# Three chained models in one kernel: masks moved between PE and DVE by batch, weights converted in another order, every step placed anew

## The chip, the cores and the metric

The kernel runs on 1 core of one Trainium2 chip. The metric is the device time of one execution in microseconds. Before the change it is 1239.44 us (median of 3 runs, 1238.56 to 1243.17).

## The reference

Attention over 4 batches, 8 heads, 576 tokens and 64 dims feeds two MLPs over the 2304 tokens. Cut to what is computed:

```python
scores = scale * np.matmul(q, k.transpose(0, 1, 3, 2))
thresh = np.max(scores, axis=-1, keepdims=True) - tau
scores = np.where(scores >= thresh, scores, -1000000000.0)
attn = np.exp(scores - np.max(scores, axis=-1, keepdims=True))
attn = attn / (np.sum(attn, axis=-1, keepdims=True) + 1e-09)
x = np.matmul(attn, v)                      # -> 2304 x 512
h = x @ w_in                                # 512 x 2048
P = a[0] + a[1] * h + a[2] * h**2 + a[3] * h**3
Q = 1.0 + np.abs(b[0]) * np.abs(h) + np.abs(b[1]) * h**2
y = (P / (Q + 1e-06)) @ w_out               # 2048 x 512
out = ((y @ w1) * (y @ w2) @ w3) @ w_out2   # 512x1024, 512x1024, 1024x1024, 1024x512
```

## The kernel before, in words

**Tiles.** Heads are taken in pairs `c` (4 to a batch). The 576 queries of a pair are cut into five blocks `blk` of 128 rows (the last holds the 64 remaining rows of both heads); `s` is the head of the pair. So a batch `b` has 36 score tiles of 128 x 576, and the kernel 144. A half `u` of a pair is blocks 0 and 1 or blocks 2 to 4.

**A score tile.** `qk` (PE, L446, L441) makes the scores in PSUM, `top` (DVE, L455) their row maximum, `thr` (DVE, L462) the threshold. The mask is then made in one of two ways. By PE: `below` (ACT, L469) writes a large Relu for each score under the threshold, `drop` (PE, L476) subtracts it in PSUM by two matmuls with the constant `minus`, and `exp` (ACT, L491) exponentiates and sums. By DVE: `exp` (ACT, L486) exponentiates everything, and one DVE instruction (L488) compares, multiplies and sums. `MASK = (1, 3)` gives blocks 1 and 3 of every batch to DVE, the others to PE. `recip` (POOL L502, then DVE L504) makes the factor 1/sum. `p_hi` and `p_lo` split the probabilities into two float16 parts `hl`: for `s == 1` ACT first multiplies by the factor (L509), a copy rounds and a plain subtraction, mostly on POOL (L301), gives the rest; for `s == 0` rounding and subtraction carry the factor, and the subtraction is then a scalar_tensor_tensor on DVE (L298). `p_t` transposes both parts by DMA, `pv` (PE, L545) multiplies by V.

**Weights.** The 72 weight tiles come in as 64-bit floats. `conv_w` makes float32 of a tile in three DVE instructions (L621, L624, L627). `split_w` makes two float16 parts of the tiles of `w_in`, `w_out`, `w1`, `w2` and of W. W is `w3` times `w_out2`, made once: `w_product` (PE, L873) for each of 8 row tiles from all 8 tiles of `w_out2` (`wo2`) and two of `w3`.

**MLPs.** The 2304 rows are 9 groups of 256. For each group `mlp1` runs 8 steps: `h_product` (PE, L761), `act_h` (ACT), `num` (DVE, L780, L782), `den` (POOL), `inv` (ACT), `quotient` (DVE, L798 to L802, last part POOL), `y_product` (PE, L818). The group's end is `y_evac` and `square` of y (ACT, L679, `sq<-yf`). `mlp2` runs 4 steps of `ab_product` (PE, L925), `a_copy`, `c_mul` (L937), `o_product` (PE, L957). The ninth group is made of the last 64 queries of each batch.

**Order.** Every step is an event with a number, in the order in which `merge` lists them. `ORDER`, a string of event numbers, says in which order the events' instructions are emitted; a generator event is resumed at each further mention of its number, and a letter behind a number gives an engine (`a` ACT, `p` POOL, `v` or none DVE) where there is a choice. Each engine executes its own instructions in this order and waits at semaphores for the others. DMAs are all issued by SP. Buffers are few: 2 score tiles `S` in PSUM (a third of batch 0's scores use `y` as well), 2 of `h`, 1 of `y`.

Of the kernel before, what the change touches and what calls it, by code (L numbers as in the profile page):

```python
# [36 lines left out]
96 158 99a 130 139 110 139 101p 98 112 139 109 102 142 110 169 144 112 134 144 113 132a 113 135 120
137 138 237 150 140 150 141 143 150 115a 145 161 180 161 153 155 116 161 118 120a 239a 172 121p 238
172 164 172 166 123 146 183 245 183 175 160 183 177 148 162 253 163 186 149 149 188 165 151a 188 156
191 152 124 156a 191 154 167 157p 168 167 126a 159 168 187 194 126 194a 170 189 197 194p 170 190  # L40
197a 171a 192 197p 176 173 199 184 176a 199v 174 240 199p 193 178v 202 196 240 179 195 202p 240 200
198 202p 185v 260 205 214 205a 241 215 201 205p 217 243 218 208 203 181 203 208a 204v 206 209 208p
209a 248 207 248 182a 211p 210 182 248 210a 212 213 210p 268 250 213v 255 213p 220 255 216 220 216a
255 242 222 216p 276 219 222 219a 244 223 258 219p 223 246 225a 247 229 226 221 228 229a 221v 263
221p 224 231v 224a 263 233 227 224p 263 227a 230 227p 283 266 230v 230p 232 232a 235 232p 234 235a
271 271 271 278 291 278 249 235p 278 251 252 286 298 236a 286 254 256 236 286 257 270 293 306 273
293 259 292 281 259 261v 318 262 265 265a 272 264 288 274 267p 277 275 293 279 269 277 313 296 279
402 294 280 406 280 295 282a 301 412 301 287 284 412 287a 297 301 289p 285 308 299 321 303 308 290
300 308 302 320 316 329 311 316 302 316 304a 322 336 319 305 323 307 315 325 324 327 324 328 330 324
333 332 331 393 331 326 348 331 335 339 344 334 339 370 337 337 339 338a 350 317a 396 343 413 340  # L50
343a 352 342 341 345p 346 346 395 346 398 351 353 400 372 349 404 373 355 406 406 309 357 355 375
310 357 312 310 354 358 401 354 376 347 314a 354 405 403 314 414 358 356 436 360v 425 407 362 365
436 365a 359 363 410 410 378 367p 415 410 380 368 380 417 381a 418 383 421 385 410 422 409 410 424
426 429 428 432 446 416 434 471 449 416 434 450 435a 452 441 473 441a 438 411a 443p 475 439 419 455
419 456 505 455 477 456 416 479 440 458 359 507 359 423p 440 458 444 407 361 407 361a 460p 508 386
364 388 361p 511 364a 388 390 366 408 408 364p 366a 445 408 369 366p 369a 462 437 371 512 463 444
369p 371a 374 391v 391 371p 374a 461 377 374p 377a 461 379 377p 379a 420 420 420 448 382 379p 382a
384 382p 384a 387 387a 384p 389 389a 431 431 431 459 387p 392 392a 389p 394 394a 392p 397 397a 394p
399 399a 442 442 442 453 470 453 453 465 482 465 465 476 493 476 476 487 504 487 397p 487 466 499
497 466a 499 399p 480 499 467p 514 510 572 510 517 518 510 483 469 427 520 483 583 427 484v 486 500a  # L60
430 488 522 500 524 539 430 532 440 525 430 563 447p 525 464 528v 501 515 529 533 430p 541 531 533a
515 542 451 535p 545 546 565 515 548 546 451 548 503a 515 567 464 550 454 569 550 454 552a 597 454
521a 570 577 558 454p 490 577 558a 491 577 573 494 491 559p 589 544 527 589 574 433 464 537 589 433
496a 472p 553 590 496 433 556 574 474 576v 594 579 474 468 580 594 468 562 478 478 594 591a 478 599
478p 594 601 603 591 604 457 457 600a 538 611 538 605 457 538 607 582 549 622 586 549 584 549 584
555 587a 657 587 555 555 659a 555 659 481 651 560a 617 617 481 566 617 628 481 662 628 485 628 485
690 509 489 489 492 509 489 492 495p 608 513 610 634 612 593 516 516 498 595p 634 498 614 502 634
502 513 615 513 502 519p 629 502v 615 506 618a 631 506 523 632 624 620 506 523 635 634 621 624a 526
636 625p 526 638 534 526 639a 627 636 526p 534 645 638 557 656 536 641 656 536 530 540 536 530 540
543p 641 656 642a 530 667 648 701 557 644 547 667 646 547 648p 665 661 649p 667 561 673 551 561 725  # L70
# [164 lines left out]
def tile_attention_mlps(  # L235
# [258 lines left out]
    def by_dve(blk):  # L494

        return blk in MASK

# [673 lines left out]
```

## Time and profile before

| | |
|---|---|
| median of the runs | 1239.44 us |
| the profiled execution's own time | 1243.93 us |
| its span | 1242.2 us |
| busy: PE, DVE, ACT, POOL | 1011.8 (81%), 898.0 (72%), 756.1 (61%), 445.4 us (36%) |
| granted TensorE clock, mean | 0.912 of 2.4 GHz |
| moved by DMA | 120.37 MB, mean 97 GB/s |

The busy shares are means over a program whose stages differ: the first has weights to convert, the last has only MLP work. So the rows below cut the span at the ends of MLP1 groups, which can be found in the trace (`sq<-yf` on ACT) and in the order of the steps.

### The profile page before, as it was taken

To read this page: it belongs to the slowest core of one execution; us is meant where nothing else is said; L and a number is where in the kernel's file an instruction comes from. 1 tells how busy PE (TensorE), PEld (TensorE's weight loads), DVE (VectorE), ACT (ScalarE), POOL (GpSimd) and SP (SyncE) were. 2 spreads that over 40 slices of the span, in tenths; PEclk is the share of its full clock that TensorE was granted. 3 is DMA by queue.
4 is the path that set the end of the run, shared out by engine and by line. 5 is a ranking of instruction groups with operands and counts; after the bars stand their busy time and mean duration, and the time that the engine had idled before them with its cause. 6 is when DMAs were issued, how large, how long until landed. Compare 5 with 4: busy or idle time off the path is not lost. (4 is left out here: it accounts for less than half of the span.)

```text
span 1242.2 us, 20722 instructions
## 1 busy us (share of the span) xinstructions
PE 1011.8 (81%) x7940; PEld 748.2 (60%) x7940; DVE 898.0 (72%) x1623; ACT 756.1 (61%) x1266; POOL 445.4 (36%) x425
## 2 busy tenths in 40 slices
PE   2463553998987767579999888799989999999997
PEld 1232432565565545357767766687767777878774
DVE  5899979868897989988858767974388533756710
ACT  5587784555767767677766555664467544544521
POOL 1145155223242644445433433443234321423311
PEclk9855665999998878779999989999999999999998
DMA  7875855635643246533481334123323331000000
GB/s 213 257 186 150 219 137 174 168 87 139 161 122 73 63 111 149 133 76 72 81 207 47 84 80 109 30 53 71 71 56 64 65 67 29 2 18 18 1 18 17
DMA packets 201443, 120.37 MB, mean 97 GB/s; under 512 B 176384, under 2 KB 180480, under 8 KB 201344
## 3 DMA queue, kind: packets, MB, share of 16 engines
q1 hardware_dynamic: 201344, 119.05, 39.1%
q8 instruction: 62, 1.02, 0.4%
q14 instruction: 37, 0.30, 0.1%
HBM read 69.21 MB, written 7.34 MB: 62 GB/s over the span
## 5 line engine op out<-in xcount | busy, mean ns | idle before, releaser
L818 PE MATMUL y<-gg,wp 128*128 128x256 f16 x1728 | 212.7, 280 | 32.2 <-POOL gg L301 17.4
L818 PEld LDWEIGHTS <-wp 128*128 128x128 f16 x1728 | 171.0, 100 | 71.7 <-issue 48.1
L761 PE MATMUL h<-xp,wp 128*128 128x256 f16 x1536 | 187.2, 282 | 30.0 <-DVE U L782 19.3
L761 PEld LDWEIGHTS <-wp 128*128 128x128 f16 x1728 | 172.8, 101 | 63.0 <-DVE U L782 21.5
L925 PEld LDWEIGHTS <-wp 128*128 128x128 f16 x1728 | 169.5, 98 | 32.4 <-issue 5.9
L301 POOL TENSOR_TENSOR A<-A,r 128x512 f32<-128x512 f32 x71 | 96.0, 1352 | 130.3 <-ACT r L775 124.4
L301 POOL TENSOR_TENSOR gg<-A,r 128x512 f16<-128x512 f32 x61 | 84.8, 1390 | 126.9 <-DVE A L802 108.8
L446 PE MATMUL S<-raw 64*128 64x288 f32 x472 | 106.2, 492 | 28.7 <-ACT p L491 15.5
L301 POOL TENSOR_TENSOR hl<-p,hl 128x576 f16<-128x576 f32 x62 | 86.6, 1397 | 119.5 <-ACT hl L285 92.4
L455 DVE TENSOR_REDUCE m<-S 128x1 f32<-128x576 f32 x132 | 95.6, 748 | 27.7 <-PE S L446 15.9
L957 PE MATMUL y<-wp,gg 128*128 128x512 f16 x432 | 102.7, 384 | 4.0 <-POOL gg L301 1.9
L301 POOL TENSOR_TENSOR gg<-U,gg 128x512 f16<-128x512 f32 x36 | 42.9, 1191 | 151.0 <-ACT gg L285 140.6
L502 POOL TENSOR_SCALAR su<-su 128x2 f32<-128x2 f32 (+1 forms) x80 | 25.0, 313 | 200.7 <-ACT p L491 137.7
L446 PEld LDWEIGHTS S<-raw 64*128 64x128 f32 x472 | 57.7, 215 | 61.1 <-ACT p L491 20.1
L768 ACT ACTIVATE U<-h,cf 128x512 f32<-128x512 f32 x72 | 55.7, 773 | 58.6 <-PE h L761 27.0
L925 PE MATMUL h<-yy,wp 128*128 128x256 f16 x768 | 91.0, 277 | 0.1
L298 DVE SCALAR_TENSOR_TENSOR hl<-p,su,hl 128x576 f16<-128x576 f32 x80 | 79.0, 988 | 15.4 <-ACT hl L287 14.6
L469 ACT ACTIVATE x<-S,th 128x576 bf16<-128x576 f32 x73 | 51.4, 735 | 44.9 <-DVE th L462 41.7
L301 POOL TENSOR_TENSOR wp<-cw,wp 128x512 f16<-128x512 f32 x53 | 72.7, 1388 | 13.2 <-ACT wp L285 6.2
L798 DVE SCALAR_TENSOR_TENSOR gg<-U,cf,r 128x512 f16<-128x512 f32 x72 | 59.5, 827 | 20.8 <-ACT r L792 20.0
L957 PEld LDWEIGHTS <-gg 128*128 128x128 f16 x432 | 41.4, 99 | 51.4 <-issue 5.2
L624 DVE SCALAR_TENSOR_TENSOR cw<-rw,cw 128x512 int32<-128x512 int32 x72 | 69.2, 962 | 2.1
(185 smaller groups left out, 1947.7 us busy)
## 6 DMA issues: line engine op xcount, KB each, us to landing
rw<-in_moe_w_dram SPq DMA_DIRECT2D x32, 512.0 KB, 4.3
rw<-in_moe_w_out_dram SPq DMA_DIRECT2D x24, 512.0 KB, 3.9
raw<-in_k_dram SPq DMA_DIRECT2D x32, 288.0 KB, 3.8
wr<-in_v_dram SPq DMA_DIRECT2D x16, 576.0 KB, 4.5
rw<-in_moe_w_in_dram SPq DMA_DIRECT2D x16, 512.0 KB, 4.4
wr<-in_v_dram SPq DMA_DIRECT2D x16, 320.0 KB, 4.5
out_dram<-A SPq DMA_DIRECT2D x16, 256.0 KB, 2.1
raw<-in_q_dram SPq DMA_DIRECT2D x16, 160.0 KB, 3.4
```

What stands on the lines that cost most here:

```text
L298: nc.vector.scalar_tensor_tensor(o, x, scale, hi, op0=ALU.mult, op1=ALU.subtract)
L301: (nc.gpsimd if eng[0] == "p" else nc.vector).tensor_tensor(o, x, y, op=op)
L446: nc.tensor.matmul(t[s][:, half, :HS], x[r, o:o + 128], y[r, keys], start=True, stop=True)
L455: nc.vector.tensor_reduce(st["m", b, c, blk][:, s:s + 1], t[:, :, :HS], axis=AX.XY, op=ALU.max, negate=True)
L469: nc.scalar.activation(x, st["S", b, c, blk][s][:, :, :HS], AF.Relu, bias=st["th", b, c, blk][:, s:s + 1], scale=-BIG)
L624: nc.vector.scalar_tensor_tensor(t, r[:, :, 1], -0x40000000, t, op0=ALU.bitwise_and, op1=ALU.bitwise_or)
L761: nc.tensor.matmul(t[:, e, :], w[:, a, o:o + 128], x[:, y, c, :], start=c + i == 0, stop=c == KD - 1 and i == 2)
L768: nc.scalar.activation(u, h, AF.Identity, bias=cf[:, 15:16], scale=cf[:, 0:1])
L798: stt(p[:, 0, :], u, cf[:, 3:4], r, ALU.add, ALU.mult)
L818: nc.tensor.matmul(t[j // 2][:, j % 2, :], w[:, a, 128 * j:128 * j + 128], x[:, y, TG * e:TG * e + TG], start=f + e + i + j % 2 == 0, stop ...
L925: nc.tensor.matmul(t[:, TG * e:TG * e + TG], w[:, a, o:o + 128], x[:, y, c, :], start=c + i == 0, stop=c == KD - 1 and i == 2)
L957: nc.tensor.matmul(st["o", g][kt], x[:, a, m:m + 128], w[:, y, :], start=jp + e + i == 0, stop=jp == 3 and e == 1 and i == 2)
```

## The change

Masks: `MASK` becomes a table by batch. Batch 0 makes all masks by PE, batch 1 as before, batches 2 and 3 all by DVE. `FIRST` does the same for the factor: in batch 0 ACT multiplies it in first for both heads, elsewhere for `s == 1` as before. `thr` and the first part of `recip` go through a helper `small` that takes POOL or DVE from the letter in `ORDER`. The lists given to `merge` are cut elsewhere, and `ORDER` is new in every line: the tiles of `w_out2` and `w3` are converted first, the W products stand in batch 0, and `mlp2` of group 0 stands already beside batch 1.

```diff
 ORDER = """
-59 0 1 3 12 17 2 4 62 5 13p 62 19a 70 21 62 7 64 22 67 24 6 25 27 10 73 28 30 73 8 32 73 33 9 81 9
...
-    MASK = (1, 3)
+    MASK = ((), (1, 3), (0, 1, 2, 3, 4), (0, 1, 2, 3, 4))
+    FIRST = ((0, 1), (1,), (1,), (1,))
...
+    def small(o, i, x, y, f, g):
+        (nc.gpsimd if eng[0] == "p" else nc.vector).tensor_scalar(o, i, x, y, op0=f, op1=g)
...
-        nc.vector.tensor_scalar(th[:, 0:n], m, d1, -1.0 if by_dve(blk) else -BIG,
-                                op0=ALU.add, op1=ALU.mult)
+        small(th[:, 0:n], m, d1, -1.0 if by_dve(b, blk) else -BIG, ALU.add, ALU.mult)
...
-        if by_dve(blk):
+        if by_dve(b, blk):
...
-    def by_dve(blk):
-
-        return blk in MASK
+    def by_dve(b, blk):
+
+        return blk in MASK[b]
...
-        nc.gpsimd.tensor_scalar(su, su, 1e-9, 2.0**-14, op0=ALU.add, op1=ALU.mult)
+        small(su, su, 1e-9, 2.0**-14, ALU.add, ALU.mult)
...
-        if scaled(blk, s):
+        if scaled(b, s):
...
-    def scaled(blk, s):
-
-        return s == 1
+    def scaled(b, s):
+
+        return s in FIRST[b]
...
-    merge(attend(0, 0), wi)
-    a = attend(0, 1); n = len(a) // 2
-    merge(a[:n], wo)
-    merge(a[n:] + attend(1, 0), M((1,0), (1,1)), wa)
-    merge(attend(1, 1), M((1,2)), wb)
+    a = attend(0, 0)
+    merge(a, wa[:len(wa)-27] + wi)
+    b = attend(0, 1)
+    merge(b, wo + M((1,0)))
+    merge(attend(1, 0), M((1,1)), wa[len(wa)-27:]+wb)
     fw_()
-    merge(attend(2, 0), M((1,3),(2,0)))
-    merge(attend(2, 1), M((1,4),(2,1)))
-    merge(attend(3, 0), M((1,5),(2,2),(2,3)))
-    merge(attend(3, 1), M((1,6),(2,4),(2,5)))
-    merge(M((1,7),(2,6),(1,8),(2,7),(2,8)))
+    merge(attend(1, 1), M((1,2),(2,0)))
+    merge(attend(2, 0), M((1,3),(2,1)))
+    merge(attend(2, 1), M((1,4),(2,2)))
+    merge(attend(3, 0), M((1,5),(2,3)))
+    merge(attend(3, 1), M((1,6),(2,4)))
+    merge(M((1,7),(2,5),(1,8),(2,6),(2,7),(2,8)))
```

DVE in batch 0, before, about its third pair: subtraction with the factor (`hl<-p,su,hl`), a conversion (`cw`), a threshold, two masks (`p,su<-S,th,p`).

```order
L298 SCALAR_TENSOR_TENSOR xp<-h,xp 128x256
L504 RECIPROCAL su<-su 128x2
L455 TENSOR_REDUCE m<-S 128x1
L298 SCALAR_TENSOR_TENSOR vl<-wr,vs,vh 128x640
L298 SCALAR_TENSOR_TENSOR hl<-p,su,hl 128x576
L621 TENSOR_SCALAR cw<-rw 128x512
L624 SCALAR_TENSOR_TENSOR cw<-rw,cw 128x512
L627 SCALAR_TENSOR_TENSOR cw<-rw,cw 128x512
L462 TENSOR_SCALAR th<-m,d_86 128x2
L488 SCALAR_TENSOR_TENSOR p,su<-S,th,p 128x576 x2
```

DVE in batch 0 now, about its third pair as well.

```order
L628 SCALAR_TENSOR_TENSOR cw<-rw,cw 128x512
L300 SCALAR_TENSOR_TENSOR xp<-h,xp 128x256
L631 SCALAR_TENSOR_TENSOR cw<-rw,cw 128x512
L508 RECIPROCAL su<-su 128x2
L460 TENSOR_REDUCE m<-S 128x1
L460 TENSOR_REDUCE m<-y 128x1
L306 TENSOR_SCALAR th<-m,d_86 128x2
L625 TENSOR_SCALAR cw<-rw 128x512
L651 TENSOR_REDUCE acc<-h 128x1
```

Subtractions and masks are gone from DVE here; maxima, some thresholds and the conversions are left.

POOL in batch 0, before, from its first instruction on data (`raw` is q; `su` the sums, `hl` the subtraction).

```order
L291 TENSOR_SCALAR raw<-raw,flag 128x256
L502 TENSOR_SCALAR su<-su 128x2
L301 TENSOR_TENSOR hl<-p,hl 128x576
L502 TENSOR_SCALAR su<-su 128x2
L301 TENSOR_TENSOR hl<-p,hl 128x576
```

POOL at the same place now (`th` the thresholds, `qp` the last queries).

```order
L293 TENSOR_SCALAR raw<-raw,flag 128x256
L303 TENSOR_TENSOR hl<-p,hl 128x576 x2
L306 TENSOR_SCALAR su<-su 128x2
L303 TENSOR_TENSOR hl<-p,hl 128x576
L306 TENSOR_SCALAR th<-m,d_86 128x2
L291 CAST hl<-p 128x576
L303 TENSOR_TENSOR hl<-p,hl 128x576 x3
L306 TENSOR_SCALAR th<-m,d_86 128x2
L433 COPY qp<-raw 64x64 x2
```

The subtractions of both heads have come to POOL, and thresholds stand between them.

PE beside batch 2, before: `ab_product` matmuls with a `drop` of two tiles among them.

```order
L925 MATMUL h<-yy,wp 128x256
L476 LDWEIGHTS minus
L476 MATMUL S<-x,minus 128x288
L476 LDWEIGHTS minus
L476 MATMUL S<-x,minus 128x288
L476 LDWEIGHTS minus
L476 MATMUL S<-x,minus 128x288
L476 LDWEIGHTS minus
L476 MATMUL S<-x,minus 128x288
L925 LDWEIGHTS wp
```

PE beside batch 2 now: a `qk` of two tiles among `ab_product` matmuls, and no `drop` anywhere in batches 2 and 3.

```order
L929 LDWEIGHTS wp
L929 MATMUL h<-yy,wp 128x256
L451 MATMUL S<-raw 128x288 x4
L929 LDWEIGHTS wp
L929 MATMUL h<-yy,wp 128x256
```

The four `drop` matmuls of a pair of tiles have left PE's queue; DVE's L492 (L488 before) stands for them.

## Rows read from the trace of the kernel before

**Rows 1.** Timeline of ACT near 555 us: start, duration, instruction.
```profile
555.36 1.06 ACT L679 ACTIVATE sq<-yf 128x1024 bf16<-128x1024 f32 x1
```

**Rows 2.** Busy time by stretch; the header row names the columns.
```profile
core 0: us, PE busy (x) PEld busy (x) DVE busy (x) ACT busy (x) POOL busy (x), PEclk, DMA share, GB/s
0.00:555.40 555.40, 373.51 (x2462) 249.94 (x2463) 474.71 (x865) 374.06 (x652) 212.63 (x209) 0.82 0.57 146
555.40:1242.30 686.90, 638.25 (x5478) 498.24 (x5478) 423.34 (x759) 382.02 (x615) 232.79 (x216) 0.98 0.25 57
```

**Rows 3.** The same view, cut at ends of MLP1 groups.
```profile
425.90:555.40 129.50, 90.98 (x682) 66.11 (x679) 116.40 (x215) 90.74 (x154) 61.89 (x55) 0.80 0.48 117
...
724.40:843.40 119.00, 107.23 (x938) 83.38 (x939) 88.92 (x158) 74.75 (x123) 43.74 (x41) 0.96 0.31 69
843.40:975.70 132.30, 125.86 (x1090) 96.25 (x1087) 81.47 (x155) 80.22 (x131) 44.76 (x47) 0.99 0.29 64
975.70:1103.10 127.40, 125.28 (x1103) 100.59 (x1102) 64.49 (x118) 63.13 (x98) 38.39 (x35) 1.00 0.16 35
```

**Rows 4.** Groups by form, DVE: count | busy us, mean ns | idle before.
```profile
L455 DVE TENSOR_REDUCE m<-S 128x1 f32<-128x576 f32 x132 | 95.6, 748 | 27.7 <-PE S L446 15.9 <-PE S L441 10.1 <-PE y L446 1.5
L298 DVE SCALAR_TENSOR_TENSOR hl<-p,su,hl 128x576 f16<-128x576 f32 x80 | 79.0, 988 | 15.4 <-ACT hl L287 14.6
...
L780 DVE SCALAR_TENSOR_TENSOR U<-h,cf,U 128x512 f32<-128x512 f32 x72 | 53.7, 746 | 21.0 <-ACT A L772 12.4 <-ACT r L775 3.7 <-ACT U L768 3.2
...
L488 DVE SCALAR_TENSOR_TENSOR p<-S,th,p 128x576 f32<-128x576 f32 x59 | 46.8, 812 | 2.4 <-ACT p L486 1.3
...
L462 DVE TENSOR_SCALAR th<-m,d 128x2 f32<-128x2 f32 x64 | 23.2, 363 | 1.5
L291 DVE TENSOR_SCALAR hl<-p,su 128x576 f16<-128x576 f32 x24 | 22.8, 951 | 1.1
...
L298 DVE SCALAR_TENSOR_TENSOR vl<-wr,vs,vh 128x640 f16<-128x640 f32 x16 | 16.9, 1054 | 6.9 <-ACT vh L287 6.9
...
L301 DVE TENSOR_TENSOR gg<-A,r 128x512 f16<-128x512 f32 x11 | 14.6, 1327 | 0.4
...
L301 DVE TENSOR_TENSOR hl<-p,hl 128x576 f16<-128x576 f32 x2 | 3.3, 1642 | 0.0
```

**Rows 5.** Groups by form, DVE: the three conversion lines.
```profile
L624 DVE SCALAR_TENSOR_TENSOR cw<-rw,cw 128x512 int32<-128x512 int32 x72 | 69.2, 962 | 2.1
...
L627 DVE SCALAR_TENSOR_TENSOR cw<-rw,cw 128x512 int32<-128x512 int32 x72 | 61.4, 853 | 1.6
...
L621 DVE TENSOR_SCALAR cw<-rw 128x512 int32<-128x512 int32 x72 | 43.6, 605 | 2.3 <-DMA rw<-in_moe_w_out_dram 1.1 <-DMA rw<-in_moe_w_dram 0.7 <-DMA rw<-in_moe_w_in_dram 0.2
```

**Rows 6.** The same three lines asked for one by one: minimum/median/maximum ns.
```profile
L621 DVE TENSOR_SCALAR cw<-rw x72: 407/421/1500, 8.1 to 523.6; 128x512 int32<-128x512 int32 x72
L624 DVE SCALAR_TENSOR_TENSOR cw<-rw,cw x72: 677/693/3336, 8.6 to 524.0; 128x512 int32<-128x512 int32 x72
L627 DVE SCALAR_TENSOR_TENSOR cw<-rw,cw x72: 668/691/1649, 9.3 to 524.7; 128x512 int32<-128x512 int32 x72
```

**Rows 7.** Groups by form, POOL.
```profile
L301 POOL TENSOR_TENSOR hl<-p,hl 128x576 f16<-128x576 f32 x62 | 86.6, 1397 | 119.5 <-ACT hl L285 92.4 <-issue 17.9 <-DMA out_dram<-A 5.8
...
L289 POOL CAST wp<-cw 128x512 f16<-128x512 f32 x5 | 3.7, 747 | 0.4 <-ACT cw L667 0.3
```

**Rows 8.** Groups by form, PE, from 800 to 1000 us.
```profile
L925 PE MATMUL h<-yy,wp 128*128 128x256 f16 x384 | 44.1, 273 | 0.0
...
L446 PE MATMUL S<-raw 64*128 64x288 f32 x88 | 13.7, 429 | 0.0
L545 PE MATMUL h<-pT,vh 128*64 128x256 f16 x108 | 7.0, 275 | 1.3 <-DVE U L782 1.3
L476 PE MATMUL S<-x,minus 128*128 128x288 bf16 x30 | 5.3, 287 | 0.0
```

**Rows 9.** Waits over the whole span: who waited for whom, us, times, longest.
```profile
PE S L446 <- ACT p L491: 15.5, 4, 14.7
```

More of the change, by code (lines that the diff above doesn't have):

```diff
@@ L37 @@
[L37 to L58, printed above, removed]
@@ L227 @@
[L227 to L230 removed]
+7 0 1 3 12 92 18 2 4 5 13v 22 8 94p 20v 10 15 24 26 27v 6 31 9 14 9 29 9 35 11a 33 17 37 17 11 39 53
+40v 16a 19 40 17 55 42 23 16 42a 48 44p 57 28 48a 59v 61 50p 46 21 63 64 21 68 66 52 21 70 96 25 32
@@ new lines @@
+2287 2297 2291p 2287 2299 2298a 2299 2287 2292 2298 2292 2292 2299 2300 2293a 2299 2293 2299 2300
+2292 2301 2307 2301 2302 2301 2302 2307 2294a 2303p 2294 2314 2308 2304 2309 2314 2304 2309 2305
+2369 2308 2305 2308 2305 2328 2310p 2305v 2315 2315 2316 2306 2315 2316 2306 2311 2317p 2311 2306
+2312 2318 2328 2312 2318 2312 2321 2319 2329 2312p 2321 2319 2329 2319 2313 2329 2330 2319p 2313
+2322 2331v 2323 2322 2313 2323 2322 2320 2330 2332 2324p 2335 2332 2325 2335 2325 2326 2342 2326
+2342 2326 2333 2336 2326p 2320 2333 2336 2333 2327 2336 2337 2327 2333p 2343 2338v 2320 2344 2343
@@ L231 @@
+2424 2412 2412a 2419 2426a 2412p 2419 2420 2421a 2425 2420 2427 2413 2422 2413 2422a 2413 2422p 2418
+2413 2418 2427a 2418 2427p 2418 2423 2423 2423 2428 2423 2428 2428 2428 2396 2430a 2429v 2429 2430
+2396 2386 2387 2387 2386 2397 2388a 2398v 2389 2397 2391 2399 2399a 2389p 2389p 2391 2399p 2401 2401
+2402 2403a 2393v 2392 2392 2402 2394 2394a 2390 2404 2394p 2390 2390 2395 2390 2395 2404a 2395 2404p
+2395 2400 2400 2400 2405 2400 2405 2405 2405 2407a 2406v 2406 2407
 """
@@ L511, in p_hi @@
         hl = T("G", [128, 2 * S], F16, name="hl")
-        copy(hl[:, 0:S], p, None if scaled(blk, s) else su)
+        copy(hl[:, 0:S], p, None if scaled(b, s) else su)
         st["hl", b, c, blk, s] = hl
@@ L517, in p_lo @@
         rest(hl[:, S:2 * S], st.pop(("p", b, c, blk, s)), hl[:, 0:S],
-             None if scaled(blk, s) else st["su", b, c, blk][:, s:s + 1])
-    def scaled(blk, s):
-        return s == 1
+             None if scaled(b, s) else st["su", b, c, blk][:, s:s + 1])
+    def scaled(b, s):
+        return s in FIRST[b]
     def p_t(b, c, blk, s):
@@ L581, in attention @@
             at(thr, b, c, blk)
-            for fn in ((exp,) if by_dve(blk) else (below, drop, exp)):
+            for fn in ((exp,) if by_dve(b, blk) else (below, drop, exp)):
                 for s in range(n):
```

363 lines of the change are left out of this document (187 added, 176 removed).

## The prediction

> **What bounds the kernel now.** I read the busy table first, then the span cut at the ends of MLP1 groups, then the groups by form. One cut serves for the whole argument: the end of MLP1's third group, `sq<-yf` at 555.4 us [rows 1]. The reader is to see two programs on its sides [rows 2]. Up to it DVE is busy 474.7 of 555.4 us, 85.5%, PE 67%, ACT 67%, POOL 38%: DVE sets the pace. Behind it PE is busy 638.3 of 686.9 us, 92.9%, DVE 61.6%: PE does. At the cut both orders have done the same of what PE waits for most: all 72 weight tiles are converted, all 8 W products made, three MLP1 groups finished. So the time is what DVE has to do before the cut over its share, plus what PE has to do behind it over its share, and I ask what the change does to each. In the finer rows [rows 3] PE's share falls as DVE's rises: PE 98% beside DVE 51%, 95% beside 62%, 90% beside 75%, 70% beside 90%.
>
> **The change, DVE before the cut.** I counted the steps of both orders down to the third `square` of y; the prices are the means of [rows 4]. Subtractions with the factor go from 41 to 16 (batch 0 has none left): 25 x 0.988 = -24.7 us. Roundings with the factor 10 to 1: 9 x 0.951 = -8.6. Masks 34 to 14 (batch 0's are on PE): 20 x 0.812 = -16.2. Maxima 76 to 67, because nine score tiles come only behind the cut: 9 x 0.748 = -6.7. Thresholds for two tiles 34 to 16, most of the rest now on POOL: 18 x 0.363 = -6.5. The first part of `recip` is new on DVE, 14 for two tiles. No row shows it there; it has the threshold's form, so 14 x 0.363 = +5.1. (Were it free it would be 0, and at the subtraction's 0.988 it would be 13.8; 8.7 us above what I take.) Two `num` steps of the fourth group slip behind the cut: 2 x 2 x 0.746 = -3.0. Two `vl` parts: -2 x 1.054 = -2.1. One plain subtraction and two last parts of `quotient` come from POOL: 1.642 + 2 x 1.327 = +4.3. Smaller things I leave out. Sum: -58.4 us, so 474.7 becomes 416.3.
>
> **What POOL gives back.** The work that leaves DVE goes in good part to POOL: 15 more subtractions x 1.397 = 21.0 us and 17 more casts of weights x 0.747 = 12.7 [rows 7], the rest about evens out: 212.6 to some 247 us, in a shorter stretch, so POOL's share goes from 38% to about 49%. That is not free for DVE. The conversion instructions have medians of 421, 693 and 691 ns with maxima of 1500, 3336 and 1649 [rows 6], and means of 605, 962 and 853 [rows 5]: most run at one speed and some wait inside for something. 72 x (184 + 269 + 162) ns is 44.3 us. If that grows as POOL's share, 44.3 x 49/38 is 57, so +13 us. If it had nothing to do with POOL it would be 0; if each added microsecond of POOL stopped DVE for one it would be 34. I take 13: 429.3 us.
> The Trainium skill speaks against this part of the change: "SBUF — State Buffer", section "Who interferes with whom", says that a DVE instruction with two SBUF inputs contends with a GpSimd instruction that reads SBUF, and that the second to issue blocks until the first is done. L624 and L627 have two SBUF inputs, L455, which reads PSUM alone, has none, and the spread of the former agrees with it; that POOL is what they wait for is not shown by a row. By the rule the full price is the rival "POOL" below; without it the first term would be 416.3.
>
> At DVE's share of before the first stretch becomes 429.3 / 0.855 = 502 us. What could take that share away: ACT does nearly what it did (374 us; ten more Relus, 17 more multiplications, fewer roundings) in 10% less time, 74%; DMA moves much the same bytes, 0.57 x 555 / 502 = 0.63; PE, 373.5 us plus ten more `drop` pairs, some 75%. None of them passes DVE. The W products, now early, are on the same side of the cut in both orders: they fill PE while it has room and enter neither term.
>
> **PE behind the cut.** `drop` matmuls 76 to 8: 68 x 5.3/30 = 0.177, -12.0 us [rows 8]. The nine tiles that come later bring 17 more `qk` matmuls, each two instructions in the trace: 34 x 13.7/88 = 5.3, and 56 more wide `pv` matmuls x 7.0/108 = 3.6. 24 `ab_product` matmuls have moved before the cut: 24 x 44.1/384 = -2.8. So 638.3 - 5.9 = 632.4 us. DVE gets 44 more masks here (30 to 74; 44 x 0.812 = 35.7), 9 maxima (6.7), 5 subtractions (4.9), about 25 `recip` parts (9.1), less 11 roundings (10.5), and some ten us of smaller pieces: 423 to about 480, that is 0.70 of a stretch of 690. At 0.70 to 0.71 I read PE's share between two rows of [rows 3]: 0.951 beside DVE 0.616 and 0.901 beside 0.747 give 0.915. 632.4 / 0.915 = 691 us.
>
> **Sum.** 502 + 691 = 1193 us of span against 1242.2. The profiled execution took 1243.93 us, 1.7 more than its span, and the median of the runs is 4.5 below it: 1193 + 1.7 - 4.5 = 1190. I forecast 1190 us, 4.0% below 1239.44.
>
> **Rivals.**
> POOL. Each added microsecond of POOL before the cut stops DVE for one: 34 instead of 13 us, 21 / 0.855 = 25 us more, 1215 us. For it: the maxima of [rows 6]. Against it: not every DVE instruction there has such a spread, and the medians stand near the minima, so most run undisturbed.
> Better packing. The new order holds DVE at 0.899 before the cut, as the stretch from 425.9 us does, and PE at 0.951 behind it, as from 843.4 us [rows 3]: 429.3 / 0.899 = 479 and 632.4 / 0.951 = 665, so, less the same 2.8, 1141 us. For it: both shares occur. Against it: the second needs DVE at 0.62, and it will have 0.70.
> Nothing gained in front. Before the cut it is not DVE's work but the chain through a score tile that sets the pace, and batch 0's chain gets longer: threshold on POOL behind a 1.4 us subtraction, Relu, two matmuls, exponential, with two or three score buffers. The stretch stays 555: 555 + 691 - 2.8 = 1243, no change. For it: PE stood at `qk` for a score buffer 14.7 us once, 15.5 us in 4 waits [rows 9]. Against it: 15.5 us is small beside the 81 us in which DVE is idle there, and DVE's maxima wait 27.7 us for scores over the whole program [rows 4].
> PE starved behind the cut, the slower side. With all masks of batches 2 and 3 on DVE, `num` and `quotient` queue behind them, and PE waits for `gg` and `U` as it does from 425.9 to 555.4 us, where it has 70% beside DVE's 90% [rows 3]. The span is back at 1242 when PE's share behind the cut is 632.4 / 740 = 0.855, and from there on the change loses; at 0.80 it is 502 + 790 - 2.8 = 1289 us. For it: these rows. Against it: DVE would be at 0.65 to 0.70 there, where rows show 0.90 and more for PE.
>
> **How the numbers follow.** Forecast 0.57; POOL 0.17; better packing 0.12; nothing gained in front 0.07; PE starved 0.07. The first three are faster: 0.86. Within 0.5% (about what a measurement of this kernel tells from no change, 6 us): 0.07. Slower: 0.07. The range: its upper end, 1228, is past POOL's 1215 by the 8.7 us of the unknown `recip` price over 0.855, 10 us, and a few more for waits, and leaves out the two rivals of 0.07; its lower end, 1150, lies between the forecast and better packing and leaves out about half of that.
>
> **What would show it.** Right: the third `sq<-yf` near 502 us with 17 DVE subtractions and roundings with the factor and 14 masks before it, DVE at 0.84 to 0.87 up to it; the conversions' means risen over 605, 962 and 853 ns at unchanged medians; behind it PE at 0.90 to 0.93 with no `drop` of batches 2 and 3, DVE near 0.70. Wrong: the third group ends later than 530 us; conversions' means unchanged (then POOL is not what they wait for) or up by a quarter (then the first rival); PE under 0.87 behind the cut with waits for DVE's `U` and `gg` at its head.

## The result, and the profile after

The changed kernel takes 1207.17 us (median of 4 runs, 1204.56 to 1209.53) against 1240.93 for the kernel before on the same chip: ratio 0.9728, 95% interval 0.9698 to 0.9757. That is 2.7% less; the forecast was 4.0%. The profiled execution took 1207.75 us with a span of 1206.0.

The timeline of ACT in the changed kernel puts the cut, the third `sq<-yf`, where [rows 1] had 555.36:

```profile
501.11 1.06 ACT L683 ACTIVATE sq<-yf 128x1024 bf16<-128x1024 f32 x1
```

Busy time by stretch, columns as in [rows 2], the changed kernel: the two sides of the cut, then two stretches that answer to [rows 3].

```profile
0.00:501.10 501.10, 352.08 (x2357) 233.06 (x2361) 438.62 (x745) 357.46 (x639) 255.47 (x236) 0.89 0.59 153
501.10:1206.00 704.90, 642.39 (x5535) 496.35 (x5532) 481.83 (x930) 375.00 (x569) 246.83 (x217) 0.99 0.28 62
...
724.80:830.20 105.40, 95.17 (x813) 73.47 (x812) 85.05 (x162) 63.13 (x96) 43.20 (x34) 0.98 0.35 76
830.20:929.20 99.00, 94.00 (x810) 73.03 (x807) 82.59 (x168) 62.44 (x95) 40.80 (x34) 1.00 0.31 63
```

In front of the cut 54.3 us went; behind it 18.0 came back. DVE is at 0.875 in front (0.855 before), PE at 0.911 behind (0.929 before). Now PE holds 0.90 and 0.95 beside a DVE at 0.81 and 0.83, where [rows 3] had 0.90 beside 0.75.

Groups by form, DVE in front of the cut, and the conversion lines asked for one by one (minimum/median/maximum ns); they answer to [rows 4 to 6]:

```profile
L628 DVE SCALAR_TENSOR_TENSOR cw<-rw,cw 128x512 int32<-128x512 int32 x72 | 68.6, 952 | 2.0
L631 DVE SCALAR_TENSOR_TENSOR cw<-rw,cw 128x512 int32<-128x512 int32 x72 | 64.0, 890 | 1.8
L625 DVE TENSOR_SCALAR cw<-rw 128x512 int32<-128x512 int32 x72 | 50.3, 698 | 7.1 <-DMA rw<-in_moe_w_in_dram 3.6 <-DMA rw<-in_moe_w_dram 2.8 <-DMA rw<-in_moe_w_out_dram 0.8
...
L300 DVE SCALAR_TENSOR_TENSOR hl<-p,su,hl 128x576 f16<-128x576 f32 x16 | 14.6, 911 | 1.4 <-ACT hl L289 1.3
L492 DVE SCALAR_TENSOR_TENSOR p<-S,th,p 128x576 f32<-128x576 f32 x14 | 10.9, 811 | 0.4 <-POOL th L306 0.2
```

```profile
L625 DVE TENSOR_SCALAR cw<-rw x72: 404/422/1501, 16.8 to 408.0; 128x512 int32<-128x512 int32 x72
L628 DVE SCALAR_TENSOR_TENSOR cw<-rw,cw x72: 669/693/1750, 17.3 to 409.4; 128x512 int32<-128x512 int32 x72
L631 DVE SCALAR_TENSOR_TENSOR cw<-rw,cw x72: 671/692/1740, 19.6 to 410.6; 128x512 int32<-128x512 int32 x72
```

The first conversion's mean rose from 605 to 698 ns and the third's from 853 to 890 at unchanged medians; the second's did not (962, 952). The two groups `hl<-p,su,hl` and `p<-S,th,p` are down to the counts of the prediction.

**What the conversions wait for.** The timeline of the changed kernel, DVE beside POOL, at two places (start, duration):

```profile
22.80 2.76 POOL L303 TENSOR_TENSOR hl<-p,hl 128x576 f16<-128x576 f32 x2 [11.84 <-ACT hl L287]
...
24.46 1.64 DVE L628 SCALAR_TENSOR_TENSOR cw<-rw,cw 128x512 int32<-128x512 int32 x1
...
61.89 1.34 POOL L303 TENSOR_TENSOR hl<-p,hl 128x576 f16<-128x576 f32 x1 [6.84 <-ACT hl L287]
...
62.01 1.50 DVE L625 TENSOR_SCALAR cw<-rw 128x512 int32<-128x512 int32 x1
```

The conversion at 24.46 ends at 26.10, 0.54 us after POOL's second subtraction (25.56); the one at 62.01 ends 0.28 us after POOL's (63.23). I went through all 216 conversions of this trace. Of the 62 that start while a POOL TENSOR_TENSOR runs, 58 end a fixed time after it: L625 0.28 to 0.29 us, L628 and L631 0.55. The other four started 0.06 us before POOL's end and ran at full speed. With no POOL instruction running at their start the means are 418, 691 and 689 ns. The kernel before shows the same: 48 of 55, at the same two distances. So a conversion that finds POOL at such an instruction stands until POOL is done. As a sum, I took for each DVE instruction in front of the cut what it lasted above the tenth percentile of its group in the whole program: 80.6 us before, 98.6 now, and 95.2 of these in instructions that start while POOL runs. The conversions hold 45.7 of the 80.6 and 54.8 of the 98.6. The largest rise is in the three instructions of `quotient`, which have two SBUF inputs as well: from 7.2 to 20.7 us. Their rows in front of the cut, before and now:

```profile
L802 DVE SCALAR_TENSOR_TENSOR A<-U,cf,A 128x512 f32<-128x512 f32 x25 | 22.5, 899 | 0.7
L798 DVE SCALAR_TENSOR_TENSOR gg<-U,cf,r 128x512 f16<-128x512 f32 x25 | 20.9, 838 | 1.5 <-ACT r L792 1.1
L800 DVE SCALAR_TENSOR_TENSOR A<-A,gg 128x512 f32<-128x512 f32 x25 | 18.1, 725 | 1.8
```

```profile
L806 DVE SCALAR_TENSOR_TENSOR A<-U,cf,A 128x512 f32<-128x512 f32 x24 | 26.0, 1085 | 0.7
L802 DVE SCALAR_TENSOR_TENSOR gg<-U,cf,r 128x512 f16<-128x512 f32 x24 | 24.2, 1008 | 0.8 <-ACT r L796 0.5 <-PE y L822 0.2
L804 DVE SCALAR_TENSOR_TENSOR A<-A,gg 128x512 f32<-128x512 f32 x24 | 22.7, 944 | 1.7
```

PE behind the cut, groups by form. First the kernel before, from 555.4 us:

```profile
L761 PE MATMUL h<-xp,wp 128*128 128x256 f16 x912 | 107.0, 276 | 9.8 <-DVE U L782 6.5 <-ACT r L775 2.5 <-DVE sc L690 0.5
...
L446 PE MATMUL S<-raw 64*128 64x288 f32 x232 | 38.8, 430 | 0.3 <-ACT raw L287 0.3
...
L545 PE MATMUL h<-pT,vh 128*64 128x256 f16 x288 | 18.7, 275 | 1.9 <-DVE U L782 1.3 <-DMA raw<-in_k_dram 0.6
L476 PE MATMUL S<-x,minus 128*128 128x288 bf16 x76 | 13.9, 287 | 1.2 <-ACT x L469 1.2
```

The same groups of the changed kernel, from 501.1 us:

```profile
L765 PE MATMUL h<-xp,wp 128*128 128x256 f16 x960 | 112.8, 273 | 14.1 <-DVE U L786 9.0 <-ACT r L779 5.2
...
L451 PE MATMUL S<-raw 64*128 64x288 f32 x264 | 48.5, 432 | 3.9 <-DVE p L492 2.1 <-POOL raw L293 1.6
...
L549 PE MATMUL h<-pT,vh 128*64 128x256 f16 x324 | 22.0, 282 | 4.9 <-DVE U L786 3.3 <-DMA pT<-hl 0.9 <-ACT U L289 0.8
...
L480 PE MATMUL S<-x,minus 128*128 128x288 bf16 x8 | 1.5, 284 | 0.8 <-ACT x L473 0.8
```

Of the drops 8 matmuls are left, 12.4 us less, and more `qk`, `pv` and `h_product` stands behind the cut than was priced: PE is busy 642.4 us there, not 632.4.

### The profile page after: what moved, and what is told of

Read it like the earlier page. It is cut to its first block, busy times and chain, and to the rows that moved or that the text cites. A ratio compares the mean times of both kernels' runs of the same rounds, so it can differ in the third digit from the quotient of the medians.

```text
span 1206.0 us, 20660 instructions
## 1 busy us (share of the span) xinstructions
PE 994.5 (82%) x7889; PEld 729.4 (60%) x7892; DVE 920.5 (76%) x1674; ACT 732.5 (61%) x1208; POOL 502.3 (42%) x452
## 5 line engine op out<-in xcount | busy, mean ns | idle before, releaser
L303 POOL TENSOR_TENSOR hl<-p,hl 128x576 f16<-128x576 f32 x81 | 114.8, 1419 | 114.5 <-ACT hl L287 107.3
L303 POOL TENSOR_TENSOR A<-A,r 128x512 f32<-128x512 f32 x67 | 88.7, 1324 | 148.5 <-ACT r L779 148.3
L303 POOL TENSOR_TENSOR gg<-A,r 128x512 f16<-128x512 f32 x64 | 89.0, 1391 | 140.5 <-DVE A L806 104.3
L490 ACT ACTIVATE p<-S,m 128x576 f32<-128x576 f32 x88 | 63.3, 737 | 40.9 <-DVE m L460 29.7
L513 ACT ACTIVATE p<-p,su 128x576 f32<-128x576 f32 x84 | 64.0, 767 | 38.1 <-DVE su L508 37.9
L802 DVE SCALAR_TENSOR_TENSOR gg<-U,cf,r 128x512 f16<-128x512 f32 x72 | 64.5, 896 | 17.3 <-ACT r L796 17.0
L772 ACT ACTIVATE U<-h,cf 128x512 f32<-128x512 f32 x72 | 55.5, 771 | 36.5 <-DVE A L806 16.3
L492 DVE SCALAR_TENSOR_TENSOR p<-S,th,p 128x576 f32<-128x576 f32 x88 | 70.0, 813 | 8.9 <-ACT p L490 6.7
L786 DVE SCALAR_TENSOR_TENSOR U<-U,cf,h 128x512 f32<-128x512 f32 x72 | 53.5, 746 | 24.7 <-ACT r L779 18.8
L804 DVE SCALAR_TENSOR_TENSOR A<-A,gg 128x512 f32<-128x512 f32 x72 | 67.3, 935 | 5.8 <-DVE gg L802 0.5
```

The lines of the kernel that those rows point to most:

```text
L303: (nc.gpsimd if eng[0] == "p" else nc.vector).tensor_tensor(o, x, y, op=op)
L492: nc.vector.scalar_tensor_tensor(x, t, st["th", b, c, blk][:, s:s + 1], x, op0=ALU.is_ge, op1=ALU.mult, accum_out=su)
L513: nc.scalar.activation(p, p, AF.Copy, scale=su)
L786: stt(u, u, cf[:, 14:15], h, ALU.add, ALU.mult)
L802: stt(p[:, 0, :], u, cf[:, 3:4], r, ALU.add, ALU.mult)
L804: stt(t, t, QC, p[:, 0, :], ALU.add, ALU.mult)
```

## The experiments

Times are medians, ratios are to the kernel before on the same chip, with 95% intervals. "Front" is the stretch up to the third `sq<-yf`, "behind" the rest of the span; stretches and waits are those of the profiled execution. Where masks were put back on another engine in an order not made for them, I placed the steps `below`, `drop` and `exp` by a rule of my own.

### Order alone, and masks alone (e1_order_only, e2_masks_only)

```diff
 # e1: the changed kernel with its new order, and
-    MASK = ((), (1, 3), (0, 1, 2, 3, 4), (0, 1, 2, 3, 4))
-    FIRST = ((0, 1), (1,), (1,), (1,))
+    MASK = ((1, 3), (1, 3), (1, 3), (1, 3))
+    FIRST = ((1,), (1,), (1,), (1,))
 # e2: the order of before with the new MASK and FIRST
```

> The new order with the masks and the factor of before (blocks 1 and 3 of each batch by DVE, the factor first for s == 1 alone): each step stands where the changed kernel has it, a drop between its Relu and its exponential. Theory 'work before the cut' (the third MLP1 group's end; DVE's work there sets the time): batch 0's 16 masks by DVE come back, 16 x 0.812 = 13 us, and 20 subtractions with the factor, 20 x 0.988 = 20 us, while POOL loses 28 us and gives back some 5; so 439 us of DVE become about 466, over 0.875 is 533 instead of 501 us; behind the cut nothing changes much (see the run with batches 2 and 3 alone). Some 1240 us, ratio to before 0.995 to 1.005. Rival 'order': the steps' places give the gain and the engine of the masks matters little: 1207 to 1215 us, ratio 0.973 to 0.980.

> The order of before with the new masks and the new factor of batch 0 (thresholds on DVE and the first part of recip on POOL as before). Theory 'work before the cut': DVE loses 16 masks and 20 subtractions before the cut, 33 us, POOL's extra 28 us cost it some 8: 475 - 25 = 450 us over 0.855 = 526 instead of 555 us; behind the cut as the run with batches 2 and 3 says, near nothing. Some 1211 us, ratio 0.973 to 0.982. Rival 'order': an order made for other engines keeps its waits, 1230 to 1250 us, ratio 0.99 to 1.01.

Measured: e1 1231.43 us, ratio 0.9919 (0.9887 to 0.9951), front 503.1; e2 1261.74, ratio 1.0159 (1.0123 to 1.0195). Busy time by stretch of e2:

```profile
0.00:573.70 573.70, 374.00 (x2490) 247.83 (x2491) 453.78 (x811) 401.46 (x706) 239.07 (x229) 0.83 0.55 142
573.70:1261.70 688.00, 629.86 (x5404) 491.31 (x5402) 447.38 (x834) 355.20 (x539) 232.77 (x216) 0.98 0.26 57
```

The front's whole gain comes with the order; behind the cut e1 takes 726.5 us, 39.6 more than the kernel before. e1's time lies between its two expectations, e2's above both of its own. Masks and factor alone lengthen the front by 18.3 us although DVE has 20.9 us less to do: work left DVE and turned into waiting (0.79 busy). Behind the cut PE has 8.4 us less to do and stands 9.5 us longer. Neither part has the change's gain by itself; together they do.

### Which masks: batches 2 and 3, batch 0 (e3_m23_old, e4_b0_old)

```diff
 # e3
-    MASK = ((), (1, 3), (0, 1, 2, 3, 4), (0, 1, 2, 3, 4))
+    MASK = ((), (1, 3), (1, 3), (1, 3))
 # e4
-    MASK = ((), (1, 3), (0, 1, 2, 3, 4), (0, 1, 2, 3, 4))
-    FIRST = ((0, 1), (1,), (1,), (1,))
+    MASK = ((1, 3), (1, 3), (0, 1, 2, 3, 4), (0, 1, 2, 3, 4))
+    FIRST = ((1,), (1,), (1,), (1,))
```

> The changed kernel with the masks of batches 2 and 3 as before (40 score tiles by Relu and two matmuls again). Theory 'PE's share falls as DVE's rises': behind the cut PE gets 80 matmuls more, 14 us (642 to 656), DVE 40 masks less, 32 us (482 to 449, 0.64 of the stretch), and PE's share goes from 0.911 back to about 0.93: 706 us instead of 705, so 1205 to 1211 us, ratio 0.971 to 0.976. Rival 'PE's work is all that counts there': 656 / 0.911 = 720, so 1220 to 1225 us, ratio 0.983 to 0.988.

> The changed kernel with the masks and the factor of batch 0 alone as before. Theory 'work before the cut': DVE 439 + 33 - 5 = 466 us before the cut, the third group ends near 533 us instead of 501, 1236 to 1242 us, ratio 0.995 to 1.001. Rival 'order': no more than 10 us, ratio 0.973 to 0.981, with the third group's end near 505 to 510 us and DVE's idle time before it shrunk.

Measured: e3 1232.37 us, 0.9935 (0.9916 to 0.9954); e4 1206.91, 0.9715 (0.9681 to 0.9748). The front of e4:

```profile
0.00:500.80 500.80, 347.44 (x2325) 231.02 (x2329) 447.95 (x794) 336.39 (x590) 230.57 (x216) 0.88 0.60 153
```

Batch 0's masks on PE and its factor on ACT are worth nothing: DVE is 9.3 us less busy in the changed kernel, POOL 24.9 us more, and the front ends at 501 in both. In e4 the rival "order" came out. e3 took longer than either expectation. There PE stood 24.3 us at `drop`, in 21 waits, so I suspected my own placing of the drops.

### The same with the drops put later (e5_m23_late, e6_order_late)

```diff
 # the order around one tile of batch 2: thr, below, drop, exp
-thr below . . drop . exp
+thr below . . . . . . . drop . . exp
```

> The changed kernel with batches 2 and 3 masked as before (TensorE adds, 88 more drops), like the run before it with this edit, but the drops and exponentials stand later in the order, so that TensorE has other work while ScalarE forms x (median distance from x to its drop 7.5 steps, as in the kernel before, where that run had 3). Theory that the engine that masks is worth little behind the cut and that the 25 us of that earlier run were TensorE standing at drops put too early: the 24 us of TensorE waiting for x fall below 8 us, and the time is 1207 to 1215 us. First rival, that each drop costs its TensorE time because TensorE bounds this stretch: 16 us of drops over the share 0.91, some 18 us, so 1222 to 1227 us with the waits gone. Second rival, that the masks' move is itself worth the 25 us (ScalarE's load, the longer hold of the score tile): 1230 us or more, with the waits gone and TensorE's share still at 0.90.

> The new order with the masks and the first factor of all batches as before, and with the drops put later as in the run beside it. If the order alone brings the change's gain: 1207 to 1215 us, the third sq<-yf at 500 to 504 us as with the new masks, and VectorE's busy time before it near 448 us. If the masks of batches 2 and 3 cost their TensorE time: as in the run beside it, 1222 to 1227 us. If neither: 1231 us as with the drops put early.

Measured: e5 1234.02 us, 0.9938 (0.9915 to 0.9960); e6 1233.25, 0.9934 (0.9906 to 0.9961). Waits of PE at `drop` behind the cut, in e3 and in e5, then the stretch behind the cut in e5, and the stretches of e6:

```profile
PE S L482 <- ACT x L475: 24.3, 21, 3.9
```

```profile
PE S L482 <- ACT x L475: 14.9, 11, 2.3
```

```profile
500.80:1232.70 731.90, 659.23 (x5614) 507.36 (x5612) 450.18 (x850) 404.85 (x649) 247.10 (x217) 0.98 0.28 60
```

```profile
0.00:502.10 502.10, 354.38 (x2328) 233.90 (x2329) 447.18 (x794) 336.59 (x590) 230.99 (x216) 0.86 0.60 153
502.10:1231.20 729.10, 656.89 (x5615) 506.21 (x5612) 449.53 (x850) 405.06 (x649) 248.09 (x217) 0.99 0.27 60
```

My theory that these masks are worth little fell: the waits at `drop` went from 24.3 to 14.9 us and the time did not. Behind the cut e5 takes 731.9 us with PE busy 659.2, the changed kernel 704.9 with 642.4. So of the 27.0 us, 16.8 are PE's work (mostly the 80 added drops: 16.7 us against 1.5) and 10.2 are PE's waiting. Between the two places tried, where the drops stand hardly matters; that DVE masks in batches 2 and 3 does. The second rival has its time, 1230 us or more, but not its condition, since the waits are not gone.

The spans now split the change. The order alone takes 11.0 us (1242.2 to 1231.2 in e6): 53.3 less in front, 42.2 more behind. Masks by DVE in batches 2 and 3 take 26.8 more (1204.4 in e4), 25.5 of them behind the cut. Batch 0's edit takes nothing (1206.0). By the medians the three are 7, 26 and 0 us.

### What POOL's reads cost DVE (e7_lo_memset, e9_lo_memset3)

Both kernels leave out the lower half of batch 0's probabilities: POOL fills it with zeros, which reads nothing, once (e7) or three times (e9).

```diff
         hl = st["hl", b, c, blk, s]
+        if b == 0:
+            st.pop(("p", b, c, blk, s))
+            for _ in range(3):              # e7: once
+                nc.gpsimd.memset(hl[:, S:2 * S], 0.0)
+            return
```

> The changed kernel, where the lower half of batch 0's probabilities is not computed: POOL fills it with zeros (a memset reads nothing) in the place of 36 subtractions of 1.39 us, of which most stand before the cut. If POOL's reads are what VectorE's two-input instructions wait for: the conversions' means fall from 698, 952 and 890 ns by some 30 to 100 ns each at unchanged medians, VectorE's busy time before the cut falls from 439 us by 8 to 20 us; and if VectorE sets the end of this stretch, the third sq<-yf comes at 485 to 494 us instead of 501 and the time is 1192 to 1202 us. If something else sets the end of it (transfers, the chain of one score tile): the means may fall, but the third sq<-yf stays at 498 to 502 us and the time at 1203 to 1209 us.

> As the run with the lower half of batch 0's probabilities filled with zeros by POOL (it took 1193.7 us, third sq<-yf at 489.2 us, first group at 268.6), but each fill is done three times: 36 x 3 x 0.58 us of POOL instead of 36 x 0.58, so that POOL is as long at each tile as in the changed kernel (1.73 us against 1.39), still without reading anything. Theory that POOL's reads block VectorE's two-input instructions: the conversions' means stay near 541, 857 and 783 ns in the first group, VectorE's busy time before the cut stays near 415 us, the third sq<-yf comes at 487 to 493 us, and the time is 1192 to 1199 us. Rival, that the run before won because POOL came free sooner and handed each tile on sooner: the third sq<-yf goes back to 498 to 506 us and the time to 1204 to 1212 us, with VectorE's busy time near 415 us and its waits for POOL longer by as much. Second rival, that any POOL instruction that uses the buffer slows VectorE, writing or reading: the conversions' means go back above 640, 920 and 850 ns.

Measured: e7 1193.72 us, 0.9606 (0.9576 to 0.9636), third group at 489.2; e9 1193.68, 0.9614 (0.9584 to 0.9645), at 490.7. The front of e9, then its conversions in the first group and those of the changed kernel:

```profile
0.00:490.70 490.70, 357.62 (x2357) 235.94 (x2361) 416.07 (x742) 357.55 (x640) 267.61 (x311) 0.87 0.60 156
```

```profile
L633 DVE SCALAR_TENSOR_TENSOR cw<-rw,cw 128x512 int32<-128x512 int32 x59 | 48.6, 823 | 1.8
L636 DVE SCALAR_TENSOR_TENSOR cw<-rw,cw 128x512 int32<-128x512 int32 x58 | 45.1, 779 | 1.6
L630 DVE TENSOR_SCALAR cw<-rw 128x512 int32<-128x512 int32 x60 | 36.3, 605 | 10.1 <-DMA rw<-in_moe_w_in_dram 4.6 <-DMA rw<-in_moe_w_dram 4.2 <-DMA rw<-in_moe_w_out_dram 1.2
```

```profile
L628 DVE SCALAR_TENSOR_TENSOR cw<-rw,cw 128x512 int32<-128x512 int32 x59 | 55.6, 943 | 1.8
L631 DVE SCALAR_TENSOR_TENSOR cw<-rw,cw 128x512 int32<-128x512 int32 x58 | 49.3, 852 | 1.6
L625 DVE TENSOR_SCALAR cw<-rw 128x512 int32<-128x512 int32 x60 | 41.3, 688 | 7.1 <-DMA rw<-in_moe_w_in_dram 3.6 <-DMA rw<-in_moe_w_dram 2.8 <-DMA rw<-in_moe_w_out_dram 0.8
```

In e9 POOL is busier than in the changed kernel (267.6 us, 255.5), yet DVE is 22.5 us less busy and the front ends 10.4 us earlier. 2.6 of the 22.5 us are three subtractions that DVE itself no longer does. So it is not POOL's time that slows the two-input conversions, but its reading. The one-input L630 is at 605 ns, below the changed kernel's 688 but above e7's 541: three fills hold it up more than one. The fills also wait for no probabilities, so how much of the earlier end comes from that is not shown. In e7 33 subtractions left POOL in front of the cut (47.6 us), and DVE's time above the tenth percentile fell from 98.6 to 76.3: 0.47 us of DVE for each of POOL's. By e4 it is 13.9 (84.7 to 98.6) for 24.9, that is 0.56.

### Fewer transfers at the start (e8_half_loads)

The kernel leaves out 12 of the first 24 weight tiles.

```diff
+        count = st["count"] = st.get("count", -1) + 1
+        if count % 2 and count < 24:
+            st["rw", key] = st["last"]
+            return
         t = T("wr", [128, 512, 2], I32, name="rw")
```

> The changed kernel, where every second one of the first 24 weight tiles is not loaded (12 x 512 KB less, its conversion reads the tile before it again). Theory that the transfers of the first 100 us (DMA share 0.88) pace the start and through it the third sq<-yf: the early groups end 8 to 20 us earlier, the third sq<-yf comes at 481 to 493 us and the time is 1187 to 1200 us. Rival, that VectorE's work bounds the whole stretch: VectorE's share in the first 100 us rises at most a little, the third sq<-yf comes at 497 to 502 us, and the time is within 4 us of 1207.

Measured: 1205.13 us, 0.9697 (0.9665 to 0.9730); the third group at 496.8. The first 100 us, of e8 and of the changed kernel:

```profile
0.00:100.00 100.00, 67.00 (x244) 32.52 (x245) 83.11 (x146) 64.30 (x123) 30.67 (x37) 0.97 0.70 194
```

```profile
0.00:100.00 100.00, 64.37 (x233) 32.15 (x235) 78.53 (x139) 60.27 (x116) 27.63 (x34) 0.98 0.88 245
```

The time is in the rival's range, the cut 0.2 us outside it: with 6 MB less to load the front is 4.3 us shorter. The transfers cost some 4 us in the first 100 us; they do not pace the front.

### The small steps (e10_small_old)

```diff
 # ORDER's letters: thr (102) to DVE; first part of recip (40) to POOL where s is the first
-40v 16a 19 40 17 55 42 23 16 42a 48 44p
+40p 16a 19 40 17 55 42 23 16 42a 48 44p
...
-25 72p 72 25 74 98 74a 36 79 100 76p 30 30 102p
+25 72p 72 25 74 98 74a 36 79 100 76p 30 30 102v
```

> The changed kernel with all thresholds on VectorE and the first part of the reciprocal's step on POOL for the first of two, as in the kernel before. Theory that these small steps are worth nothing that can be measured, since VectorE's busy time before the cut can change by 9 us (batch 0's masks) without moving it: 1203 to 1212 us. Rival, that each waits behind POOL's 1.4 us subtractions on the chain from maximum to exponential, or that 18 x 0.36 us of VectorE count in full: 1213 to 1220 us, or, if POOL's queue is what delays thresholds in the changed kernel, 1195 to 1202 us.

Measured: 1215.51 us (1213.70 to 1216.80), 0.9787 (0.9758 to 0.9816). Waits of DVE in front of the cut:

```profile
DVE su L508 <- POOL su L306: 15.2, 13, 3.9
```

I had expected nothing; it is 8.3 us by the medians, 7.3 by the ratios. The reciprocal's first part is a 0.2 us step on POOL, but there it queues behind 1.4 us subtractions, and DVE stood 15.2 us for it; in the changed kernel DVE stands 8.5 us at the same step, for ACT. The front is 3.3 us longer, the rest 3.4. The run moves thresholds and reciprocals together, so what each of them costs is not shown.

### Late MLP1 work from POOL to DVE (e11_late_dve, e12_late_dve_q)

```diff
 # letters of ORDER. e11: den and quotient's last part, groups 6 to 8; e12: quotient's last part, groups 3 to 8
-1989 1950 1981 1989 1950 1992 2033 1981p 2006
+1989 1950 1981 1989 1950 1992 2033 1981 2006
```

> The changed kernel, where the 19 sums of den and 23 last products of quotient that POOL does in MLP1's last three groups are VectorE's (0.69 us instead of 1.3 to 1.4 us each); VectorE is busy only 0.47 of that stretch. Theory that the waits at the head of TensorE's queue cost their time there: the 6.5 us of y waiting for POOL's gg after 929 us fall below 2 us and the stretch from 929 us to the end shortens by 3 to 7 us, 1200 to 1204 us. Rival, that TensorE's work fills these waits another way or that VectorE's own queue (num, masks) takes their place: within 2 us of 1207, or slower by up to 5 us.

> The changed kernel, where the last products of quotient are VectorE's in all of MLP1's groups from the fourth on (45 x 0.69 us on VectorE instead of 45 x 1.38 us on POOL); den stays on POOL. Between the cut and 929 us VectorE is busy 0.82, so 30 x 0.69 = 21 us more make it 0.87. If POOL's latency is what TensorE's y waits for (16.3 us of waits behind the cut): the waits fall to 4 us or less and the time to 1194 to 1202 us. If TensorE's share falls as VectorE's rises, whoever does the product, as the rows of the kernel before suggested: waits for VectorE's U and gg grow by as much, and the time is 1204 to 1214 us.

Measured: e11 1201.13 us (1200.33 to 1202.53), 0.9673 (0.9645 to 0.9701); e12 1208.24 (1207.11 to 1210.58), 0.9731 (0.9702 to 0.9761). The last three groups in the changed kernel and in e11, then PE's waits behind the cut in e12:

```profile
929.20:1206.00 276.80, 251.69 (x2122) 196.69 (x2120) 129.74 (x237) 103.02 (x152) 65.91 (x57) 1.00 0.10 24
```

```profile
926.50:1198.50 272.00, 252.35 (x2122) 197.45 (x2119) 134.85 (x264) 102.58 (x151) 30.03 (x30) 0.99 0.11 24
```

```profile
PE y L821 <- DVE gg L302: 14.8, 15, 2.1
PE h L764 <- DVE U L785: 11.9, 10, 2.8
```

Where DVE is half idle, its shorter instruction (0.7 instead of 1.3 to 1.4 us) takes 4.8 us out of that stretch; e11 beats both kernels, by about 6 us the changed one. e12 brings DVE to 0.835 between the cut and 935 us. Behind the cut PE then waits 14.8 us for DVE's `gg`, nearly as long as the 16.3 us for POOL's in the changed kernel, and nothing is gained.

## Why the prediction was right, and where it was not

**The signs** came out: 17 subtractions and roundings with the factor and 14 masks in front, PE at 0.911 behind (0.90 to 0.93 forecast), DVE at 0.684 (near 0.70), and two of the three conversions' means risen. The reasons behind them held less well.

**First term, 502 us forecast, 501.1 measured.** The number is right by luck, its reason is not. DVE's busy time fell by 36.1 us; with the 18.0 given back to POOL that is 54.1 of work, against the 58.4 of the sum. So DVE stood at 438.6, not 429.3. (Summed by instructions, some 61 us of work left. A mean duration is too high a price, because neighbouring DVE instructions overlap: by 38.7 us in front before, by 30.8 now.) The step "At DVE's share of before" failed in the other direction: 0.875, not 0.855, and the two errors cancel.

e6 and e4 show what the sum could not: with the new order and the old masks DVE is busy 447.2 us and the front ends at 502.1. Of the order's 53.3 us, 27.5 are work of DVE and 25.8 its idle time (80.7 to 54.9), a share of 0.891. That is close to the front half of the rival "Better packing" (0.899), which I gave 0.12; its other half, 0.951 behind, did not come. (429.3 / 0.899 is 478 there, not 479.) Of the 58.4 us, 49.5 were subtractions, roundings and masks, which I put down to batch 0's edit. By count, 20 subtractions and 16 masks, 32.8 us, go with that edit, the rest with the order. By e4 the edit takes 9.3 us from DVE, 23.2 less the 13.9 that POOL gives back, and adds 9.6 us of idle time, so it moves the cut not at all. For this edit the rival "Nothing gained in front", which I gave 0.07, had the outcome; that batch 0's longer chain is the reason is not shown, as the idle time is spread over many waits. DVE bounds this stretch only together with what feeds it; dividing by a fixed share made idle time look like work.

**What POOL gives back, 13 us forecast, 18.0 measured**, with the mechanism now shown by e7 and e9; the rival "POOL", one for one, was too dear (0.47 to 0.56). The 13 us were priced for the conversions alone, which rose by 9.1. `quotient`'s three instructions, in no term, rose by 13.5, and the subtractions and roundings, now fewer, fell by 6.0. POOL grew by 42.9 us in front, not 34. The Trainium skill, "SBUF — State Buffer", section "Who interferes with whom", says that the second to issue blocks until the first is done, and that a DVE instruction with two SBUF inputs contends only with a GpSimd instruction that reads. The trace agrees on both: the fixed 0.55 us after POOL's end, and in e9 28 two-input conversions that start beside a running memset at 691 and 689 ns. The one-input L630 is held up by a memset too: the 8 that start with 0.3 us or more of one left last 595 to 784 ns and end 0.28 to 0.29 us after it. The same page of the Trainium skill, section "SBUF: two separate sides", has that for instructions in a two-port mode, and no run here shows whether L630 is in one. What I left open as "not shown by a row" could have been read before: the distance from POOL's end to the conversion's end, in the timeline.

**Second term, 691 us forecast, 704.9 measured: the step that failed.** "638.3 - 5.9 = 632.4" came out as 642.4; 10.0 over 0.915 is 11 us, and the share, 0.911, is 3 more. `drop` was right (12.0; 12.4 measured). The nine tiles that come later were priced too low: `qk` from 38.8 + 10.1 to 48.5 + 12.0, 11.6 instead of 5.3, with 40 instructions instead of 34, and `pv` 6.9 instead of 3.6 over all its forms. Two `h_product` steps of the fourth group, 5.8 us, I had not seen slip behind the cut. In the other direction, 82 `ab_product` matmuls ran before the cut, not 24: 9.5 us instead of 2.8. With small changes elsewhere these make some 6 of the 10 us; for the rest, the groups' busy times add up to 678 us in both kernels, and PE's own is smaller by their overlap, which shrank by 4 us. I took a mean from 800 to 1000 us [rows 8]; the rows for the whole stretch would have given `qk` 7.9 us, still short of 11.6.

**PE starved**, the slower side, did not come: PE waits 16.3 us for POOL's `gg` behind the cut (8.1 before) and 9.5 for DVE's `U`, and holds 0.90 and more beside a DVE of 0.82. [Rows 3] had been read as a rule that PE's share falls with DVE's; in the new order it does not: e5 has DVE at 0.615 behind the cut and PE at 0.901.

**The sum.** 17 us between 1190 and 1207: 14 from the second term, 1 back from the first, and 4 from the step from span to median, where I subtracted 2.8 and 1.2 are to be added.

**What is left open.** The value of masks depends on the order around them (27 us behind the cut in the new order, none in the old), and in the old order I placed the steps; an order made for those masks might do better. Which part of the order gives the 25.8 us of idle time was not tried alone. The granted clock in front was 0.82 before, 0.86 in e6 and 0.89 in the changed kernel; whether that has a part in DVE's shorter idle time is not shown either.

## What to carry to other kernels

Before work is moved from DVE to POOL, look in the timeline for DVE instructions that end a fixed time after a POOL instruction: here each microsecond of POOL's reading took 0.47 to 0.56 from DVE, so a 1.4 us subtraction on POOL costs DVE some 0.7 to 0.8 us (an estimate from these two) and saves little of the 0.8 to 1.0 it takes there. Ask this of every DVE instruction with two SBUF inputs, not only of those whose spread caught the eye. Don't divide a bound engine's remaining work by its old share: take work away in one experiment and see whether the end moves or only the idle time. Count what slips past your cut on the other side by where each engine stands at that time: the order of steps gave 24 `ab_product` matmuls in front, the trace 82.

## What the runs showed of the hardware

A DVE conversion held up by POOL's TENSOR_TENSOR ends 0.28 us (one SBUF input, 0.42 us alone) or 0.55 us (two, 0.69 alone) after POOL's end. POOL is held up the other way: its `hl<-p,hl` takes 1.27 us alone and up to 1.85, and of the 33 in the changed kernel that start while a DVE instruction with two SBUF inputs runs, 28 end 1.13 to 1.14 us after it. DVE instructions that read PSUM with one SBUF input were never held up: 88 masks last 803 to 819 ns, 72 of L786 733 to 749, beside a POOL that is 42% busy.
